# A gated mix of a spectral filter and a token MLP: mirrored filter rows read backwards by DMA, full-height matmuls, spectrum renumbered

## The chip, the cores and the metric

The kernel runs on one core of a Trainium2 chip. The metric is the device time of one execution in microseconds (us). The kernel before took 139.53 us, the median of three runs that lay between 139.4 and 141.93 us. The profile that is read below is of one execution of 138.61 us, of which 136.6 us are the span that the profile covers.

TensorE (PE) does the matmuls; "PEld" is its weight load, which runs beside the matmuls. VectorE (DVE) and ScalarE (ACT) do the element work. SyncE (SP) issues nearly all DMAs, and its queue of issues is called SPq. The DMAs run on 16 DMA engines.

## The reference: what is computed

The input x has 2048 tokens of 512 features. Three things are made of it and mixed:

```python
def _A_ref(x, w_r, w_i):                       # spectral filter
    X = rfft2(x)                               # 2048 x 257 complex
    X = X * (w_r + 1j * w_i)                   # w_r, w_i: 2048 x 257
    return irfft2(X, s=(2048, 512))

def _B_ref(x, w1, b1, w2, b2):                 # MLP over the tokens
    h = layernorm(x)                           # over the features
    u = gelu(einsum("bsd,sf->bdf", h, w1) + b1)     # 2048 -> 1792
    return (einsum("bdf,fs->bds", u, w2) + b2).transpose(0, 2, 1)

g = sigmoid((x * gate_w).sum(-1, keepdims=True))
out = g * _A_ref(x, A_w_r, A_w_i) + (1 - g) * _B_ref(x, ...)
```

## The kernel before

**A planner writes the order.** The kernel records tasks with `add(engine, duration, emit, reads, writes, prio, ...)`. Class `Plan` then simulates them with its own estimated durations and emits the instructions of every engine in the order that comes out. On the chip each engine works strictly through its own list, so the order is fixed, whatever the true times are. An instruction that waits holds up everything behind it in its engine's list.

**MLP.** The first matmul (`m1`, line 652) multiplies w1, which arrives in three parts: one of 6 column tiles (`wa`) and two of 4 column tiles (`wb`), each loaded by four DMAs. ACT applies gelu (line 666). The second matmul (`m2`, line 927) needs all 14 tiles of w2, which are loaded into the same buffers by seven DMAs of 1 MB. The m2 matmuls also fill PE's time around the spectral stages.

**Spectral filter.** The transform over the tokens is done by matmuls with cosine and sine tables (`fa`, lines 509 to 512) and radix-4 butterflies on DVE; the transform over the features by `fb` (lines 617 to 620), whose results ACT copies into `B` (line 624). Frequency k and its mirror 2048 - k are made from the same matmul results, so the filter is needed at both, side by side.

**The filter W.** `W` in SBUF holds 128 partitions x (real/imaginary, 2 kinds of rows `lt`, 4 blocks `e`, 2 places: computed and mirrored) x 257 values. `ld_W` loads the computed rows to their places. The mirrored rows run the other way, so they are loaded in forward order to a staging tile `wt`. PE then turns them with an anti-diagonal matrix (`wf`, line 702, 16 matmuls of 256 columns, and `wfn`, line 712, 4 small ones for the last column), and ACT copies them to `W` (lines 706 and 715). `wprep` on DVE (lines 722 to 726) waits for both components of W, and everything after it on DVE is in this order: small products (`c0b`), the butterfly `bfly` (765), a special line `nyq` (746 to 749), the multiplication by W (`mul`, 773), `comb`, `ob`, and the inverse radix-4 steps (548 to 564). Row 0 of the spectrum and the row at the Nyquist frequency are special and sit on partition 0; eight rows of them travel through a small matmul (`linem`, line 804).

**Inverse and output.** `i1` (lines 835 to 842) transforms back over the tokens, `i3` (lines 909 to 913) over the features. In both, one matmul of each group contracts a single row, from partition 0: line 841 (`d(1)[0:1]` against `ti[0:1]`, 4 times) and line 910 (`zv[0][0:1, 1]` against `g[0:1]`, 16 times). The bias matmuls (631, 633) contract 14 and 4 rows, and `linem` 9. ACT and DVE finish each group of 128 tokens, and SP stores it.

**Queues.** All loads of W, w1's second and third part and w2 stand in one queue, SP's, in this order: gate weights, W real (12 DMAs), the third part of w1 (4 DMAs of 512 KB), W imaginary (12 DMAs), the inverse table `ti`, the table `tg`, w2 (7 DMAs). SP uses eight DMA semaphores in turn: before it issues a DMA it waits until the one issued eight before has landed.

Of the kernel before, what the change touches and what calls it, by code (L numbers as in the profile page):

```python
# [16 lines left out]
P = 128  # L17
# [13 lines left out]

def ti_at(r):
    return (0, 1024, 512, 1920)[r], (512, 896)[r % 2]


def make_tables():
# [10 lines left out]
    for r in range(4):  # L47
        s = 4 * p + r
        for n, k0 in enumerate((0, 2)):
            th = ang(s, k0 + 4 * np.arange(64), S)  # L50
            ta[:, r, n * 128:n * 128 + 64] = np.cos(th)
            ta[:, r, n * 128 + 64:n * 128 + 128] = -np.sin(th)
        ta[:, r, 64] = alt
        th = ang(s, 1 + 4 * p, S)
        ta[:, r, 256:384] = np.cos(th)
        ta[:, r, 384:512] = -np.sin(th)
        ta[:, r, 512:640] = -np.cos(th)

        k = np.where(p < 64, 4 * p, 2 + 4 * (p - 64))
        o, w = ti_at(r)  # L60
        v = ti[:, o:o + w]
        if r % 2:
            sg = np.where(p < 64, 1.0, -1.0)[:, None]
# [6 lines left out]
            v[0, 2:4] = alt * (0.5 ** 0.5 if r == 1 else -(0.5 ** 0.5))  # L70
            th = ang(1 + 4 * p, s, S)
            v[:, 4] = -np.sin(th)
            v[:, 5] = np.cos(th)
            v[:, 6] = np.sin(th)
            ti[:, o:o + w] = v.reshape(P, w)
        else:
            s5 = np.append(s, 512)
            for lt, kk in enumerate((k, 1 + 4 * p)):
                th = ang(kk, s5, S)
                c, n = np.cos(th), -np.sin(th)  # L80
                if lt == 0:
                    n[0, 0:P] = 0.0 if r == 0 else -alt
# [4 lines left out]
    ti[0, 2816:2945] = np.append(alt, 1.0)  # L87
# [174 lines left out]
def kernel(  # L262
# [42 lines left out]
    def alloc_first():  # L305
# [8 lines left out]
        V.memset(t["warm"], 0.0)  # L314
        t["st"] = sb([P, 4096], BF16, "st")
        t["gl"] = sb([P, NFT, D], BF16, "gl")
        t["W"] = sb([P, 2, 2, 4, 2, WL], BF16, "W")
        t["wn"] = sb([1, 2, WL], BF16, "wn")
        t["ta"] = sb([P, 4, 640], BF16, "rot")
        t["wt"] = sb([P, 2, 2, 4, WL], BF16, "wt")  # L320
# [62 lines left out]
    def ld_bias():  # L383
        t["b1b"] = sb([NFT, P], BF16, "b1b")
        t["b2b"] = sb([4, D], BF16, "b2b")
        dma(t["b1b"][:], B_b1.rearrange("(t f) -> t f", f=P))
        dma(t["b2b"][:], B_b2.rearrange("(q n) -> q n", q=4))
    add("SP", 1.0, ld_bias, writes=["bias"], prio=7.1, nbytes=16384)
# [21 lines left out]
    def ld_W(comp):  # L410
        v = wsrc[comp].rearrange("(e c k) l -> c e k l", e=4, k=4)
        z = wsrc[comp].rearrange("(v u w) l -> w u v l", v=4, u=2)

        def emit():
            W, u = t["W"], t["wt"]
            dma(W[:, comp, 1, :, 0, 0:257], v[:, :, 1, :])
            dma(u[:, comp, 1, :, 0:257], v[:, :, 3, :])
            dma(W[1:64, comp, 0, :, 0, 0:257], v[1:64, :, 0, :])
            dma(W[64:128, comp, 0, :, 0, 0:257], v[0:64, :, 2, :])
            dma(u[64:127, comp, 0, :, 0:257], v[65:128, :, 0, :])  # L420
            dma(u[0:64, comp, 0, :, 0:257], v[64:128, :, 2, :])

            for i in range(2):
                dma(W[0:1, comp, 0, 2 * i:2 * i + 2, 0, 0:257], z[0:1, i, 0:2, :])
            dma(u[127:128, comp, 0, 0:2, 0:257], z[0:1, 1, 2:4, :])
            dma(u[127:128, comp, 0, 2, 0:257], wsrc[comp][1536:1537, :])
            dma(u[127:128, comp, 0, 3, 0:257], wsrc[comp][0:1, :])
            dma(t["wn"][:, comp, 0:257], wsrc[comp][1024:1025, :])
        return emit

    for comp in range(2):
        add("SP", 9.0 - 2 * comp, ld_W(comp), writes=[("W", comp), ("wt", comp)], prio=17 + 8 * comp, nbytes=300000, after=[a0])
        if comp == 0:
            load_wb(1)
# [8 lines left out]
    for r in range(4):  # L443
# [128 lines left out]
    def sp0():  # L572
        V.tensor_copy(t["sp"][:], t["X"][:, 0, :, :, :, 0])
# [25 lines left out]
    add("DVE", 0.15, lambda: V.tensor_copy(t["X"][:, 0, :, :, :, 0], t["fx"][:]), reads=["fx"],  # L599
# [94 lines left out]
    for comp in range(2):  # L694
        for lt in (1, 0):
            for a in range(2):
                tag = ("fa", "fb")[a]

                def wf(comp=comp, lt=lt, a=a, tag=tag):
                    pw = t["pw", comp, lt, a] = ps([P, 2, L], F32, tag, 2)  # L700
# [6 lines left out]
                add("ACT", act(512), wfe, reads=[("pw", comp, lt, a)], writes=[("W~", comp, lt)], prio=3, free=[tag])

    def wfn():
        pw = t["pwn"] = ps([P, 4, 4], F32, "fa", 2)  # L710
        for e in range(4):
            T.matmul(pw[:, e], lhsT=t["flip"][:], rhs=t["wt"][:, :, :, 3 - e, 256], start=True, stop=True)
    add("PE", mm(*[4] * 4), wfn, reads=[("wt", 0), ("wt", 1), "flip"], writes=["pwn"], prio=5, alloc=["fa"])
    wtk = [("W~", comp, lt) for comp in range(2) for lt in range(2)]
    add("ACT", 0.3, lambda: A.copy(t["W"][:, :, :, :, 1, 256].rearrange("p k a e -> p (k a) e"), t["pwn"][:].rearrange("p e k -> p k e")),
        reads=["pwn"], writes=wtk, prio=3, free=["fa"])

    pbk = [("pb", lt, e, c) for lt in range(2) for e in range(4) for c in range(2)]

    def wprep():  # L720
        W, pm = t["W"], t["wpm"]
        V.tensor_scalar_mul(W[0:1, :, 0, 0, :, 0:257], W[0:1, :, 0, 0, :, 0:257], 0.5)
# [4 lines left out]
    add("DVE", 0.8, wprep, reads=[], writes=[("W", 0), ("W", 1), "wpm"] + wtk, prio=1)  # L727


    for lt in range(2):  # L730
# [8 lines left out]
        if lt == 0:  # L739
            def nyq():  # L740
                pz = sb([1, 1280], F32, "X")
                na = pz[:, 0:1024].rearrange("p (i v l) -> p i v l", i=2, v=2)
                nn = t["nn"] = pz[:, 1024:1280].bitcast(BF16).rearrange("p (v l) -> p v l", v=2)
                wn, v = t["wn"], t["B"][0:1, 0, 0, 2:4, :]
# [4 lines left out]
                V.tensor_mul(nn[:, :, 0], t["c0"][0:1, 0, 0, 1, :], wn[:, 0, 0:257:256])  # L749
# [18 lines left out]
        for comp in range(2):  # L768
# [5 lines left out]
            add("DVE", tt(4096), mul, reads=["xs", ("W", comp), ("W~", comp, lt)], writes=[("pp", "st")[comp]], prio=pr)  # L774
# [19 lines left out]
        if lt == 0:  # L794
            def lines():
                t["s9"] = sb([9, D], BF16, "s9")
                t["s8"] = sb([8, D], BF16, "s8")
                dma(t["s9"][0:8], t["B"][0:1, 0].rearrange("p e (c v) l -> p (e c) (v l)", c=2))
# [9 lines left out]
    for lt in range(2):  # L808
# [5 lines left out]
        if lt == 0:  # L814
            add("SP", 0.5, lambda: dma(t["B"][0:1, 0].rearrange("p e (c v) l -> p (e c) (v l)", c=2), t["s8"][:]),
                reads=["s8"], writes=[("T", 0, 0), ("T", 0, 1)], prio=0, nbytes=8192)

    for h in range(2):
        for r in (0, 2, 1, 3):
            for lt in range(2):  # L820
                tag = ("fa", "fb")[lt]

                def i1(h=h, r=r, lt=lt, tag=tag):
                    if "zz" not in t:
                        t["zz"] = sb([P, 2, 2, 2, 2, 4, P], BF16, "X")
                        t["ze"] = sb([P, 2, 2, 2, 2, L], BF16, "wt")
# [3 lines left out]
                    for v in range(2):  # L830
# [5 lines left out]
                        else:  # L836
# [3 lines left out]
                            if n > P:  # L840
                                T.matmul(p1[:, v, 0:n], lhsT=d(1)[0:1], rhs=t["ti"][0:1, 2816:2945], start=False, stop=True)
# [58 lines left out]
    for grp in groups:  # L900
        for j in grp:
# [3 lines left out]
            def i3(j=j, q=q, r=r, tag=tag):  # L905
# [4 lines left out]
                T.matmul(p3[:, 0, 0:129], lhsT=zv[0][0:1, 1], rhs=g[0:1, 512:641], start=False, stop=True)  # L910
# [99 lines left out]
```

## Time and profile before

| what | value |
|---|---|
| median of three runs | 139.53 us |
| the profiled execution | 138.61 us |
| its span | 136.6 us |
| PE busy | 130.8 us (96%) |
| DVE busy | 114.6 us (84%) |
| ACT busy | 82.5 us (60%) |
| DMA | 23.18 MB, mean 170 GB/s |
| clock granted to PE | full in every stretch |

How to read the views that follow. The line with 40 digits gives the busy share of an engine in 40 equal slices of the span (3.4 us each), in tenths. The chain of work starts at the last instruction and goes back, at each step, to what released it; each piece has its start, its length and its line. A window row gives, for a stretch of the span, its length, the clock granted to PE (1.00 is full), the mean busy share of the 16 DMA engines, and GB/s. The share of the DMA engines can exceed 1 where packets of one engine overlap. In the list of groups, a matmul's "mean ns of one" is its latency; as matmuls are pipelined, the time that one costs PE is the distance from its start to the next start, which the chain shows.

### The profile page before, as it was taken

How to read it: one execution, taken by the hardware profiler on the slowest of the kernel's cores; microseconds unless marked ns; L12 is line 12 of the kernel's file. 1: busy time of each engine (PE TensorE's matmuls, PEld its weight loads, DVE VectorE, ACT ScalarE, POOL GpSimd, SP SyncE). 2: the span in 40 equal slices, each digit the busy share in tenths (PEclk: the TensorE clock that was granted, in tenths of full speed). 3: DMA queues.
4: the chain of work that ended last, by engine and by line, in shares of the span. 5: the costliest groups of instructions: out<-in, count | busy, mean ns of one | idle time of the engine just before them, and what ended most of it. 6: DMA issues, size and time to landing. Idle time of an engine off the chain costs nothing.

```text
span 136.6 us, 2166 instructions
## 1 busy us (share of the span) xinstructions
PE 130.8 (96%) x763; PEld 71.8 (53%) x777; DVE 114.6 (84%) x291; ACT 82.5 (60%) x159; POOL 0.2 (0%) x4
## 2 busy tenths in 40 slices
PE   6988999999999999999999999999999999999991
PEld 2353555445544857444445455557755545555590
DVE  0999999999999983699999999994885999949531
ACT  4066699999999999972220072259956457553200
POOL 0000000000000000000000000000000000000000
PEclk9999999999999999999999999999999999999999
DMA  4999999992899479999128600000000030303031
GB/s 124 318 376 362 361 364 349 332 166 42 243 348 258 81 255 281 413 409 404 47 19 350 247 0 5 2 2 0 0 0 5 0 154 14 139 5 154 6 112 38
DMA packets 17110, 23.18 MB, mean 170 GB/s; under 512 B 1078, under 2 KB 14540, under 8 KB 17100
## 3 DMA queue, kind: packets, MB, share of 16 engines
q1 hardware_dynamic: 16540, 22.39, 50.9%
q10 hardware_dynamic: 560, 0.66, 1.4%
q8 instruction: 6, 0.10, 0.3%
q14 instruction: 4, 0.03, 0.1%
HBM read 20.93 MB, written 2.10 MB: 169 GB/s over the span
## 4 chain that ended last, share of the span: by engine, by line
PE 62%; DMA 25%; SPq 9%; issue 1%; DVE 0%
PE acc L927 34%; PE acc L652 13%; DMA wa<-in_B_w_dram 11%; SPq L303 9%; DMA wt<-in_A_w_i_dram 8%; DMA wt<-in_A_w_r_dram 5%; PE fa L835 1%; PE fb L835 1%; PE fa L927 1%; PE fb L911 1%; PE fa L911 1%; PE fb L910 1%; PE fa L910 1%; PE fa L842 1%; PE fa L620 1%
## 5 line engine op out<-in xcount | busy, mean ns | idle before, releaser
L927 PE MATMUL acc<-gl,wb 128*128 128x512 bf16 (+1 forms) x123 | 30.9, 372 | 0.3
L652 PE MATMUL acc<-h,wb 128*128 128x512 bf16 x124 | 29.0, 379 | 0.1
L927 PE MATMUL acc<-gl,wa 128*128 128x512 bf16 (+1 forms) x94 | 23.4, 372 | 0.1
L947 ACT ACTIVATE x<-acc,ombb,omg 128x512 bf16<-128x512 f32 x14 | 10.7, 778 | 16.9 <-PE acc L927 16.9
L927 PEld LDWEIGHTS <-wb 128*128 128x128 bf16 x136 | 14.9, 114 | 9.9 <-issue 0.2
L652 PEld LDWEIGHTS <-wb 128*128 128x128 bf16 x128 | 12.4, 98 | 13.1
L652 PE MATMUL acc<-h,wa 128*128 128x512 bf16 x62 | 16.8, 379 | 1.0 <-DMA wa<-in_B_w_dram 0.5
L927 PEld LDWEIGHTS <-wa 128*128 128x128 bf16 x102 | 11.5, 114 | 8.8
L652 PEld LDWEIGHTS <-wa 128*128 128x128 bf16 x96 | 9.1, 98 | 10.1 <-DMA wa<-in_B_w_dram 0.6
L666 ACT ACTIVATE gl<-acc,b1f 128x512 bf16<-128x512 f32 x12 | 8.6, 715 | 8.4 <-PE acc L652 8.3
L458 DVE BATCH_NORM_STATS2 stats<-x 128x6 f32<-128x512 bf16 x16 | 10.7, 672 | 2.4 <-DMA x<-in_A_x_dram 2.4
L482 ACT ACTIVATE h<-x,nmr,rstd 128x512 bf16<-128x512 bf16 x13 | 9.8, 805 | 1.2 <-DVE nmr L473 1.2
L515 ACT CAST X<-fa 128x512 bf16<-128x512 f32 x16 | 8.8, 583 | 2.6 <-PE fa L512 2.5
L680 ACT ACTIVATE x<-x 128x512 bf16<-128x512 bf16 x16 | 10.2, 673 | 0.0
L652 PE MATMUL fb<-h,wa 128*128 128x512 bf16 x31 | 9.0, 379 | 0.0
L953 DVE TENSOR_TENSOR x<-x,eo 128x512 bf16<-128x512 bf16 x14 | 5.4, 418 | 2.7 <-ACT x L947 2.7
L348 PE MATMUL fa<-xp 128*128 128x512 bf16 x13 | 5.7, 632 | 1.2 <-DVE xp L314 1.2
L918 ACT ACTIVATE eo<-fa,g 128x512 bf16<-128x512 f32 x8 | 5.5, 686 | 2.1 <-PE fa L913 1.2
L918 ACT ACTIVATE eo<-fb,g 128x512 bf16<-128x512 f32 x8 | 5.5, 688 | 0.0
L806 ACT CAST s<-fa 8x512 bf16<-8x512 f32 x1 | 0.6, 575 | 7.8 <-PE fa L804 7.8
L624 ACT CAST B<-fb 128x512 bf16<-128x512 f32 x8 | 5.3, 661 | 0.0
L624 ACT CAST B<-fa 128x512 bf16<-128x512 f32 x8 | 5.2, 650 | 0.0
(164 smaller groups left out, 235.5 us busy)
## 6 DMA issues: line engine op xcount, KB each, us to landing
wb<-in_B_w_dram SPq DMA_DIRECT2D x8, 512.0 KB
wb<-in_B_w_dram SPq DMA_DIRECT2D x4, 1024.0 KB
wa<-in_B_w_dram SPq DMA_DIRECT2D x3, 1024.0 KB
wa<-in_B_w_dram SPq DMA_DIRECT2D x3, 768.0 KB
x<-in_A_x_dram SPq DMA_DIRECT2D x3, 512.0 KB
out_dram<-x SPq DMA_DIRECT2D x3, 512.0 KB
rot<-dft_ti SPq DMA_DIRECT2D x1, 736.5 KB
rot<-dft_ta SPq DMA_DIRECT2D x4, 160.0 KB
```

The lines of the kernel that those rows point to most:

```text
L303: (eng or nc.sync).dma_start(out=out_ap, in_=in_ap)
L348: T.matmul(pw[:], lhsT=t["warm"][:, 0:P], rhs=t["warm"], start=True, stop=True)
L458: V.bn_stats(out=t["stats"][:, j, :], in_=t["x"][:, j // 4, j % 4, :])
L482: add("ACT", act(512, 2), lambda j=j: A.activation(t["h"][:, j // 4, j % 4, :], t["x"][:, j // 4, j % 4, :], ActF.Identity, bias=t["nmr"][ ...
L515: add("ACT", act(512), lambda r=r, dq=dq: A.copy(t["X"][:, :, r, :, dq, :], t["pa", r, dq][:]), reads=[("pa", r, dq)], writes=[("X", r, dq ...
L624: A.copy(t["B"][:, lt, e, 2 * c:2 * c + 2, :].rearrange("p s (i b) -> p s i b", b=4), t["pb", lt, e, c][:].rearrange("p s b i -> p s i b"))
L652: T.matmul(t["u", ft][:], lhsT=w[:, j // 4, j % 4, c * P:(c + 1) * P], rhs=t["h"][:, j // 4, j % 4, :], start=(j == jorder[0]), stop=(j == ...
L666: gelus.append(add("ACT", act(512, 1), lambda ft=ft: A.activation(t["gl"][:, ft, :], t["u", ft][:], ActF.Gelu_apprx_tanh, bias=t["b1f"][:, ...
L680: A.activation(t["x"][:, q, r, :], t["x"][:, q, r, :], ActF.Copy, accum_out=t["glog"][:, 4 * q + r:4 * q + r + 1])
L918: A.activation(t["eo", j][:], t["i3", j][:], ActF.Copy, scale=t["g"][:, j:j + 1])
L927: T.matmul(t["y", j, n][:, cs], lhsT=w[:, o, 512 * q + r:512 * q + 512:4], rhs=t["gl"][:, ft, cs], start=(ft == 0), stop=(ft == NFT - 1))
L947: A.activation(tbuf(j).rearrange("p h d -> p (h d)"), t["y", j, 0][:], ActF.Identity, bias=t["ombb2"][:, j:j + 1], scale=t["omg"][:, j:j + 1])
```

## The change

Four edits go together.

1. **The mirrored rows are read backwards by DMA into their place.** `wt`, the 20 turning matmuls and the 9 ACT copies are gone. `ld_W` now issues four loads of 63 or 64 rows by 4 blocks, and eight loads of 128 rows whose source is written as 2 groups of 64 rows with a negative step (`"(o i) l -> o i l", o=2` and `[:, ::-1]`; `"(i q) l -> q i l", q=4` and `[0:4:2, ::-1]`). In the built program the source of such a load is [2 entries][64 rows, step -4 rows][257 values] and its destination [128 partitions][257 values]. There are 16 DMAs for each component in `ld_W` where there were 12, and two more for each component (`special`), which write two rows at partition 64 over what the backward loads put there. In SP's list these stand behind `ti` and `tg`, and the last two behind the first 1 MB of w2.
2. **The spectrum is renumbered**, so that a backward run of rows starts on partition 0 or 64: the tables are made for the new numbering (`KA`, `KB`, `p ^ 64`), and the special row moves from partition 0 to 64.
3. **Full-height matmuls.** The matmuls that contracted 1, 4, 9 or 14 rows contract all 128; the other rows of the operands are zero, for which three tiles are cleared at the start (`s9`, `b1b`, `b2b`, three DVE memsets).
4. `ze`, which lived in the staging tile's memory, has memory of its own.

```diff
+        t["s9"] = sb([P, D], BF16, "s9")
+        t["b1b"] = sb([P, P], BF16, "b1b")
+        t["b2b"] = sb([P, D], BF16, "b2b")
+        for k in ("s9", "b1b", "b2b"):
+            V.memset(t[k][:], 0.0)
...
         def emit():
-            W, u = t["W"], t["wt"]
-            dma(W[:, comp, 1, :, 0, 0:257], v[:, :, 1, :])
-            dma(u[:, comp, 1, :, 0:257], v[:, :, 3, :])
-            dma(W[1:64, comp, 0, :, 0, 0:257], v[1:64, :, 0, :])
-            dma(W[64:128, comp, 0, :, 0, 0:257], v[0:64, :, 2, :])
-            dma(u[64:127, comp, 0, :, 0:257], v[65:128, :, 0, :])
-            dma(u[0:64, comp, 0, :, 0:257], v[64:128, :, 2, :])
...
+            W, src = t["W"][:, comp], wsrc[comp]
+            dma(W[0:64, 1, :, 0, 0:257], v[64:128, :, 1, :])
+            dma(W[64:128, 1, :, 0, 0:257], v[0:64, :, 1, :])
+            dma(W[0:64, 0, :, 1, 0:257], v[64:128, ::-1, 2, :])
+            dma(W[65:128, 0, :, 1, 0:257], v[65:128, ::-1, 0, :])
+            for e in range(4):
+                dma(W[:, 1, e, 1, 0:257], v[:, 3 - e, 3, :].rearrange("(o i) l -> o i l", o=2)[:, ::-1])
+                dma(W[:, 0, e, 0, 0:257], src[512 * e + 2:512 * e + 258, :].rearrange("(i q) l -> q i l", q=4)[0:4:2, ::-1])
+            dma(W[64:65, 0, 1:3, 1, 0:257], z[0:1, 0:2, 3, :])
...
+        def special():
             for i in range(2):
-                dma(W[0:1, comp, 0, 2 * i:2 * i + 2, 0, 0:257], z[0:1, i, 0:2, :])
...
+                dma(t["W"][64:65, comp, 0, 2 * i:2 * i + 2, 0, 0:257], z[0:1, i, 0:2, :])
+        return emit, special
...
+        add("SP", 9.0 - 2 * comp, emit, writes=[("W", comp)], prio=17 + 8 * comp, nbytes=300000, after=[a0])
+        add("SP", 1.0, special, writes=[("W", comp)], prio=29.5, nbytes=4112)
...
-                    for i in range(2):
-                        T.matmul(pw[:, i], lhsT=t["flip"][:], rhs=t["wt"][:, comp, lt, 3 - 2 * a - i, 0:L], start=True, stop=True)
...
-                    A.copy(t["W"][:, comp, lt, 2 * a:2 * a + 2, 1, 0:L], t["pw", comp, lt, a][:])
...
-                T.matmul(pl8[:], lhsT=t["tb"][0:9, 1152:1160], rhs=t["s9"][:], start=True, stop=True)
+                T.matmul(pl8[:], lhsT=t["tb"][:, 1152:1160], rhs=t["s9"][:], start=True, stop=True)
...
-                                T.matmul(p1[:, v, 0:n], lhsT=d(1)[0:1], rhs=t["ti"][0:1, 2816:2945], start=False, stop=True)
+                                T.matmul(p1[:, v, 0:n], lhsT=d(1), rhs=t["ti"][:, 2816:2945], start=False, stop=True)
...
-                T.matmul(p3[:, 0, 0:129], lhsT=zv[0][0:1, 1], rhs=g[0:1, 512:641], start=False, stop=True)
+                T.matmul(p3[:, 0, 0:129], lhsT=zv[0][:, 1], rhs=g[:, 512:641], start=False, stop=True)
```

More of the change, by code (lines that the diff above doesn't have):

```diff
@@ L29, in bf @@
     return np.ascontiguousarray(a.astype(ml_dtypes.bfloat16))
+KA = np.append(0, 256 - 4 * np.arange(1, 64))
+KB = 254 - 4 * np.arange(64)
 def ti_at(r):
@@ L48, in make_tables @@
         s = 4 * p + r
-        for n, k0 in enumerate((0, 2)):
-            th = ang(s, k0 + 4 * np.arange(64), S)
+        for n, kk in enumerate((KA, KB)):
+            th = ang(s, kk, S)
             ta[:, r, n * 128:n * 128 + 64] = np.cos(th)
@@ L53, in make_tables @@
         ta[:, r, 64] = alt
-        th = ang(s, 1 + 4 * p, S)
+        th = ang(s, 1 + 4 * (p ^ 64), S)
         ta[:, r, 256:384] = np.cos(th)
@@ L57, in make_tables @@
         ta[:, r, 512:640] = -np.cos(th)
-        k = np.where(p < 64, 4 * p, 2 + 4 * (p - 64))
+        k = np.append(KB, KA)
         o, w = ti_at(r)
@@ L62, in make_tables @@
         if r % 2:
-            sg = np.where(p < 64, 1.0, -1.0)[:, None]
+            sg = np.where(p < 64, -1.0, 1.0)[:, None]
             th = ang(k, s, S)
@@ L69, in make_tables @@
             v[:, 3] = -sg * np.sin(th)
-            v[0, 2:4] = alt * (0.5 ** 0.5 if r == 1 else -(0.5 ** 0.5))
-            th = ang(1 + 4 * p, s, S)
+            v[64, 2:4] = alt * (0.5 ** 0.5 if r == 1 else -(0.5 ** 0.5))
+            th = ang(1 + 4 * (p ^ 64), s, S)
             v[:, 4] = -np.sin(th)
@@ L77, in make_tables @@
             s5 = np.append(s, 512)
-            for lt, kk in enumerate((k, 1 + 4 * p)):
+            for lt, kk in enumerate((k, 1 + 4 * (p ^ 64))):
                 th = ang(kk, s5, S)
@@ L81, in make_tables @@
                 if lt == 0:
-                    n[0, 0:P] = 0.0 if r == 0 else -alt
+                    n[64, 0:P] = 0.0 if r == 0 else -alt
                 u = v[:, 256 * lt:256 * lt + 256]
@@ L86, in make_tables @@
                     u[:, P] = c[:, P] if lt == 0 else -n[:, P]
-    ti[0, 2816:2945] = np.append(alt, 1.0)
+    ti[64, 2816:2945] = np.append(alt, 1.0)
     tb = np.zeros((P, 3, 4, 64))
@@ L317, in alloc_first @@
         t["W"] = sb([P, 2, 2, 4, 2, WL], BF16, "W")
-        t["wn"] = sb([1, 2, WL], BF16, "wn")
+        t["wn"] = sb([P, 2, WL], BF16, "wn")
         t["ta"] = sb([P, 4, 640], BF16, "rot")
-        t["wt"] = sb([P, 2, 2, 4, WL], BF16, "wt")
         t["wpm"] = sb([P, 2, 2, 4, 2], F32, "wpm")
@@ L383, in ld_bias @@
     def ld_bias():
[L384 to L388, printed above, removed]
+        dma(t["b1b"][0:NFT], B_b1.rearrange("(t f) -> t f", f=P))
+        dma(t["b2b"][0:4], B_b2.rearrange("(q n) -> q n", q=4))
+    add("SP", 1.0, ld_bias, writes=["bias"], prio=7.1, nbytes=16384, after=[a0])
     load("tb", [P, 1160], BF16, tabs["tb"], 296960, prio=9)
@@ L414, in emit @@
         def emit():
-            W, u = t["W"], t["wt"]
-            dma(W[:, comp, 1, :, 0, 0:257], v[:, :, 1, :])
-            dma(u[:, comp, 1, :, 0:257], v[:, :, 3, :])
-            dma(W[1:64, comp, 0, :, 0, 0:257], v[1:64, :, 0, :])
-            dma(W[64:128, comp, 0, :, 0, 0:257], v[0:64, :, 2, :])
-            dma(u[64:127, comp, 0, :, 0:257], v[65:128, :, 0, :])
-            dma(u[0:64, comp, 0, :, 0:257], v[64:128, :, 2, :])
-            for i in range(2):
-                dma(W[0:1, comp, 0, 2 * i:2 * i + 2, 0, 0:257], z[0:1, i, 0:2, :])
[L425 to L429, printed above, removed]
+            W, src = t["W"][:, comp], wsrc[comp]
[7 more added lines that the diff above has]
+            dma(W[64:65, 0, 1:3, 1, 0:257], z[0:1, 0:2, 3, :])
+            dma(W[64:65, 0, 0, 1, 0:257], src[0:1, :])
+            dma(W[64:65, 0, 3, 1, 0:257], src[1280:1281, :])
+            dma(t["wn"][64:65, comp, 0:257], src[1024:1025, :])
+        def special():
+            for i in range(2):
+                dma(t["W"][64:65, comp, 0, 2 * i:2 * i + 2, 0, 0:257], z[0:1, i, 0:2, :])
+        return emit, special
     for comp in range(2):
-        add("SP", 9.0 - 2 * comp, ld_W(comp), writes=[("W", comp), ("wt", comp)], prio=17 + 8 * comp, nbytes=300000, after=[a0])
+        emit, special = ld_W(comp)
+        add("SP", 9.0 - 2 * comp, emit, writes=[("W", comp)], prio=17 + 8 * comp, nbytes=300000, after=[a0])
+        add("SP", 1.0, special, writes=[("W", comp)], prio=29.5, nbytes=4112)
         if comp == 0:
@@ L510, in fa @@
                 T.matmul(pa[:, 1], lhsT=w(3), rhs=ta[:, 384:640], start=False, stop=True)
-                T.matmul(pa[:, 0, :, 0:64], lhsT=w(0), rhs=ta[:, 0:128], start=True, stop=True)
-                T.matmul(pa[:, 0, :, 64:128], lhsT=w(1), rhs=ta[:, 128:256], start=True, stop=True)
+                T.matmul(pa[:, 0, :, 64:128], lhsT=w(0), rhs=ta[:, 0:128], start=True, stop=True)
+                T.matmul(pa[:, 0, :, 0:64], lhsT=w(1), rhs=ta[:, 128:256], start=True, stop=True)
             add("PE", mm(128, 128, 256, 256), fa, reads=[("xf", r % 2), ("ta", r)], writes=[("pa", r, dq)], prio=0, alloc=["fa"],
@@ L572, in sp0 @@
     def sp0():
-        V.tensor_copy(t["sp"][:], t["X"][:, 0, :, :, :, 0])
+        V.tensor_copy(t["sp"][:], t["X"][:, 0, :, :, :, 64])
     dk = [("D", r) for r in range(4)]
@@ L598 @@
                dk + ([] if lt else ["sp"]), [("Z", lt, 0), ("Z", lt, 1)], pr, False)
-    add("DVE", 0.15, lambda: V.tensor_copy(t["X"][:, 0, :, :, :, 0], t["fx"][:]), reads=["fx"],
+    add("DVE", 0.15, lambda: V.tensor_copy(t["X"][:, 0, :, :, :, 64], t["fx"][:]), reads=["fx"],
         writes=[("Z", 0, 0), ("Z", 0, 1)], prio=3.1)
@@ L630, in biasT @@
         pb = t["pbias"] = ps([P, 32], F32, "fa", 2)
-        T.matmul(pb[:, 0:NFT], lhsT=t["b1b"][:], rhs=t["flip"][0:NFT, P - NFT:P], start=True, stop=True)
+        T.matmul(pb[:, 0:NFT], lhsT=t["b1b"][:], rhs=t["flip"][:, P - NFT:P], start=True, stop=True)
         for r in range(4):
-            T.matmul(pb[:, 16 + 4 * r:20 + 4 * r], lhsT=t["b2b"][:, r::4], rhs=t["flip"][0:4, P - 4:P], start=True, stop=True)
+            T.matmul(pb[:, 16 + 4 * r:20 + 4 * r], lhsT=t["b2b"][:, r::4], rhs=t["flip"][:, P - 4:P], start=True, stop=True)
     add("PE", 0.3, biasT, reads=["bias", "flip"], writes=["pbias"], prio=9, alloc=["fa"])
@@ L692 @@
     add("SP", 0.2, ld_ti, writes=["ti"], prio=28, nbytes=754176, after=[pl.last_w["pa", r, dq] for r in range(4) for dq in range(4)])
[L694 to L700, printed above, removed]
-                    for i in range(2):
-                        T.matmul(pw[:, i], lhsT=t["flip"][:], rhs=t["wt"][:, comp, lt, 3 - 2 * a - i, 0:L], start=True, stop=True)
-                add("PE", mm(256, 256), wf, reads=[("wt", comp), "flip"], writes=[("pw", comp, lt, a)], prio=5, alloc=[tag])
-                def wfe(comp=comp, lt=lt, a=a):
-                    A.copy(t["W"][:, comp, lt, 2 * a:2 * a + 2, 1, 0:L], t["pw", comp, lt, a][:])
[L707 to L716, printed above, removed]
     pbk = [("pb", lt, e, c) for lt in range(2) for e in range(4) for c in range(2)]
@@ L721, in wprep @@
         W, pm = t["W"], t["wpm"]
-        V.tensor_scalar_mul(W[0:1, :, 0, 0, :, 0:257], W[0:1, :, 0, 0, :, 0:257], 0.5)
+        V.tensor_scalar_mul(W[64:65, :, 0, 0, :, 0:257], W[64:65, :, 0, 0, :, 0:257], 0.5)
         ends = [W[:, comp].rearrange("p a e s l -> p (a e) s l")[:, :, :, 0:257:256] for comp in range(2)]
@@ L726, in wprep @@
         V.tensor_sub(pv[1], ends[1][:, :, 0], ends[1][:, :, 1])
-    add("DVE", 0.8, wprep, reads=[], writes=[("W", 0), ("W", 1), "wpm"] + wtk, prio=1)
+    add("DVE", 0.8, wprep, reads=[], writes=[("W", 0), ("W", 1), "wpm"], prio=1)
     for lt in range(2):
@@ L740, in nyq @@
             def nyq():
-                pz = sb([1, 1280], F32, "X")
+                pz = sb([P, 1280], F32, "X")[64:65]
                 na = pz[:, 0:1024].rearrange("p (i v l) -> p i v l", i=2, v=2)
                 nn = t["nn"] = pz[:, 1024:1280].bitcast(BF16).rearrange("p (v l) -> p v l", v=2)
-                wn, v = t["wn"], t["B"][0:1, 0, 0, 2:4, :]
+                wn, v = t["wn"][64:65], t["B"][64:65, 0, 0, 2:4, :]
                 for i in range(2):
@@ L748, in nyq @@
                 V.tensor_add(nn[:, 1], na[:, 1, 1], na[:, 0, 0])
-                V.tensor_mul(nn[:, :, 0], t["c0"][0:1, 0, 0, 1, :], wn[:, 0, 0:257:256])
+                V.tensor_mul(nn[:, :, 0], t["c0"][64:65, 0, 0, 1, :], wn[:, 0, 0:257:256])
             add("DVE", 3 * d1(512) + 0.1, nyq, reads=bk + [("W", 0), ("W", 1), ("c0", 0)] + pbk, writes=["nn"], prio=0.5)
@@ L773, in mul @@
                 V.tensor_mul(o, xs, w)
-            add("DVE", tt(4096), mul, reads=["xs", ("W", comp), ("W~", comp, lt)], writes=[("pp", "st")[comp]], prio=pr)
+            add("DVE", tt(4096), mul, reads=["xs", ("W", comp)], writes=[("pp", "st")[comp]], prio=pr)
         def comb(lt=lt):
@@ L795, in lines @@
             def lines():
[L796 removed]
                 t["s8"] = sb([8, D], BF16, "s8")
[L798 removed]
+                dma(t["s9"][0:8], t["B"][64:65, 0].rearrange("p e (c v) l -> p (e c) (v l)", c=2))
                 dma(t["s9"][8:9], t["nn"].rearrange("p v l -> p (v l)"))
@@ L814 @@
         if lt == 0:
-            add("SP", 0.5, lambda: dma(t["B"][0:1, 0].rearrange("p e (c v) l -> p (e c) (v l)", c=2), t["s8"][:]),
+            add("SP", 0.5, lambda: dma(t["B"][64:65, 0].rearrange("p e (c v) l -> p (e c) (v l)", c=2), t["s8"][:]),
                 reads=["s8"], writes=[("T", 0, 0), ("T", 0, 1)], prio=0, nbytes=8192)
@@ L825, in i1 @@
                         t["zz"] = sb([P, 2, 2, 2, 2, 4, P], BF16, "X")
-                        t["ze"] = sb([P, 2, 2, 2, 2, L], BF16, "wt")
+                        t["ze"] = sb([P, 2, 2, 2, 2, L], BF16, "ze")
                     p1 = t["i1", h, r, lt] = ps([P, 2, L], F32, tag, 2)
```

## The prediction

> **What bounds the kernel now.** I read the slices first, then the chain, then the loads of W in windows, then DVE after them.
>
> ```profile
> PE   6988999999999999999999999999999999999991
> DVE  0999999999999983699999999994885999949531
> DMA  4999999992899479999128600000000030303031
> ```
>
> PE is full from 10 us to the end, at full clock: the end is set by the sum of what PE does, so long as its fixed list never waits. DVE has one hole, in the two slices from 51 us: before it can start on the filter it waits for W.
>
> ```profile
> 103.03 0.06 PE fa L909
> 103.08 0.16 PE fa L910
> 103.24 0.16 PE fa L911
> ...
> 103.52 0.06 PE fb L909
> ```
>
> In the chain (start, length, line) a 129-column matmul costs 0.06 us; the one-row matmul of line 910 costs 0.16, and so does its full-height successor in line 911.
>
> ```profile
> 27.00:28.00 1.00, 1.00 1.22 276
> 28.00:29.00 1.00, 1.00 1.16 141
> 29.00:30.00 1.00, 1.00 1.12 171
> 30.00:31.00 1.00, 1.00 0.94 110
> 31.00:32.00 1.00, 1.00 0.38 69
> 32.00:33.00 1.00, 1.00 0.15 37
> ...
> 37.00:38.00 1.00, 1.00 1.09 379
> ```
>
> These windows (length, PE clock, DMA share, GB/s) show W's real part arriving. From 28 to 33 us, 528 KB move, which is the 1016 rows of 514 bytes of the two 63-row and two 64-row loads. The rows do not spread evenly: from 31 us on 0.38 and then 0.15 of 16 engines, 6.1 and 2.4 engines, still work while the others are empty. The shape of a load decides on how many engines it runs: 63 rows cannot be dealt out in 16 equal parts.
>
> ```profile
> 47.98 0.43 SPq L303 DMA_DIRECT2D tg<-dft_tg  x1
> 48.51 1.67 SPq L303 DMA_DIRECT2D wa<-in_B_w_dram  x3
> ```
>
> ```profile
> 52.87 0.42 DVE L722 TENSOR_SCALAR W<-W 1x1028 bf16<-1x1028 bf16 x1 [2.04 <-ACT W L715]
> ```
>
> ```profile
> 89.96 0.06 PE fa L839
> ```
>
> From the timelines of SP and DVE and from the chain: SP has issued the last of W when `tg` goes out at 47.98; `wprep` starts at 52.87; 37.1 us later, at 89.96, the inverse `i1` starts on PE. Between them DVE stands idle for 1.5 us only (two waits for `B`, 1.2 and 0.3 us).
>
> **The change, part by part.**
>
> *One-row matmuls.* At full height lines 910 and 911 should cost 0.06 each, 0.20 us less for a pair: 16 pairs give 3.2 us, the four of lines 841 and 842 0.8 us. Together 4.0 us, all behind 89.96. The bias and `linem` matmuls are six; at most 0.1 us.
>
> *Turning on PE and ACT.* The chain has a pair of L702 at 0.22 us: 8 pairs 1.8 us, and 0.09 for L712. The nine ACT copies (about 0.7 us each) go too. All this lies before 52 us.
>
> *DVE memsets.* Three at the start; the one of 256 words takes 0.27 us, so under 1 us, hidden in DVE's first wait of 2.4 us for x.
>
> *The loads of W.* This decides. As many rows as before come in, but per component 1020 of them by four loads that deal out like the old ones (64 and 63 rows), and 1024 by eight loads whose source has an outer count of 2. No such load of 128 rows is in the trace. From one side it runs on 16 engines like the old 128-row loads, from the other on 2, half of the rows on each. I take two: a count of 63 visibly kept loads from 16 engines, and 2 is the outermost count here.
>
> The Trainium skill bears on this, against the change: "DMA: Bandwidth & Descriptors", section "Why a DMA increments its semaphore by 16 and not by 1", says that a load runs on the largest number of engines up to 16 that divides the slowest dimension of both patterns. That would be 9 for 63 rows, as the tail of the windows suggests, and 2 here, always the same lowest two; by 16 engines the sum would be the second rival's.
>
> What does a row cost one engine? Where 2.4 engines were busy (32 to 33 us), each moved 37 / 2.4 = 15.4 GB/s, 33 ns a row; at 31 us 69 / 6.1 = 11.3 GB/s, 45 ns. Slowest reading: nine engines carried 56 rows of the 63-row loads and 32 of the others from 28.0 to 33.2 us, 59 ns. Fastest: the best slice of the page, 413 GB/s over 16 engines, 20 ns. I take 33 ns, from the window nearest to two engines.
>
> The two engines then work in order, as all these loads stand in one queue:
> - Start: the old 128-row loads of real W (1024 rows, 64 per engine, 2.1 us) were through by 28.0, so W begins at 25.9.
> - Four plain loads: up to 48 + 28 = 76 rows, 2.5 us: 28.4.
> - Eight backward loads: 512 rows each, 16.9 us: 45.3.
> - Third part of w1: 4 x 32 KB per engine at 379 / 16 = 23.7 GB/s, 5.5 us: 50.8. PE needs it at about 52: a wait of 1 to 3 us.
> - Imaginary W: 2.5 + 16.9 us: 70.2.
> - `ti`, `tg` and the first 1 MB of w2 (120 KB per engine, 5.1 us: 75.3), because the last `special` rows stand behind them in SP's list; about 2 us to land (`B<-s`, issued by 87.91, freed line 839 at 89.96): 77.3.
>
> So `wprep` starts at 77.3, not 52.87. SP's twelve extra issues (about 0.65 us each) vanish in its waits on the semaphore of eight before. Queued behind are w2 (7 MB, 18 us at 400 GB/s, complete by 93) and all of DVE's list.
>
> *What is late next.* DVE's stretch from `wprep` to `i1` is 37.1 - 1.5 = 35.6 us, as `B` is long ready: `i1` at 112.9. PE runs out of work at about 73 us (the first w2 matmul was at 70.2), gets w2 piecemeal, and stands until 112.9; its gain before that is lost. From `i1` to the end of the span: 136.6 - 89.96 - 4.0 = 42.6 us, since the matmuls behind `i1` stay behind it in PE's list. Span 155.5; with the 2.0 us around the span 157.5, against the profiled 138.61. The runs' median is 0.9 above that execution: 158.4, and I forecast 159, the rest for a gap or two between loads.
>
> The skill's "TensorE: Matmul & The Clock Gate", Part 1, adds that an idle PE falls to half clock until some 3.4 us of work have passed; the trace, with PE never idle, cannot show it. By it the start of `i1` would cost an estimated 1.7 us more.
>
> **Rivals.**
>
> *Same mechanism, slower rows (45 to 59 ns).* Each engine has 2 x (512 + 76) = 1176 rows, so 1 ns a row moves the end by 1.2 us: 12 ns more give 173, 26 ns more 190. For it: the 31 us window and the landing at 33.2. Against: there up to nine engines wrote into few partitions at once. *Faster rows (20 to 30 ns)* give 144 to 155; only loads with longer rows moved at that rate.
>
> *The backward loads spread over 16 engines: faster.* Place: the eight loads per component. Price: then W is through by about 48 as now, the last `special` lands behind 1 MB of w2 (4 us) at about 53, and `i1` starts at 90 again. PE saves 4.0 us behind it: 132.6 + 2.0 = 134.6, and 1.8 us from the turning become idle time. If DVE (15.15 us busy of 17 from 103 to 120) cannot follow, 137 to 139. It decides as soon as the engines per load are more than two by enough that W is in by 53; at two engines even 20 ns a row leaves `wprep` at 62, nine us late. For it: 128 rows stand on the destination's side.
>
> *Full height does not remove the 0.16 us:* 4 us on top of any case.
>
> **How the numbers follow.** Two engines at 30 to 45 ns a row, 155 to 173: 0.62. Slower rows, 173 to 190: 0.15. Faster rows, 144 to 155: 0.10. Spread loads: 0.13, of which 0.08 faster and 0.05 within 2%. A difference of 2% is about what runs of this kernel can tell from none (they spread from 139.4 to 141.93). The range 146 to 183 leaves out the spread loads and the ends of the other two.
>
> **What would show it.** Right: DMA digits of 1 or 2 at 30 to 60 GB/s in two stretches of some 17 us (about 28 to 45 and 53 to 70); `wprep` waiting for a DMA until about 77; PE empty in places from 73 to 113; lines 910 and 911 at 0.06 in the chain; full DVE for 36 us from `wprep`. Wrong: W complete by 50 with DMA digits of 9, or a backward load that takes much less than 64 x 33 ns = 2.1 us; then the answer is the spread case.

## The result and the profile after

The changed kernel took 159.45 us, the median of four runs (157.18 to 159.83), beside 140.11 us for the kernel before in four runs. The ratio is 1.131, with a 95% interval of 1.109 to 1.154: slower. Ratios here are taken over the runs that lie near the fastest of each kernel, so they can differ from the ratio of the medians beside them. The profiled execution took 159.64 us, with a span of 157.8 us.

The slices of the changed kernel's page, each 3.9 us long:

```profile
PE   6889999999999500000599999999999999999991
DVE  3989999999999000000319999999994968999981
PEclk9999999999999975555579999999999999999999
DMA  5999999611179711179994007600000000303321
```

PE was full to the end before. Now it has one hole, from 53 to 77 us, and is full again behind it; DVE's hole lies in the same place. DMA has two stretches of the digit 1, one per component of W. PE's clock falls to half in the hole.

The windows of the changed kernel (length, PE clock, DMA share, GB/s):

```profile
31.00:42.00 11.00, 1.00 0.15 38
46.00:48.00 2.00, 1.00 1.08 360
55.00:67.00 12.00, 0.60 0.15 37
56.00:57.00 1.00, 1.00 0.16 36
57.00:58.00 1.00, 0.67 0.15 37
58.00:59.00 1.00, 0.50 0.15 36
...
81.00:82.00 1.00, 0.88 1.03 422
```

A share of 0.15 is 2.4 of 16 engines, as in the one window of the kernel before where the other engines were empty. The share counts packets that overlap, so it is no count of engines. The trace also keeps the semaphore updates that DMAs make as they land: in this kernel a two-group load has two, a 63-row load nine, and in the kernel with one run of 128 rows (below) each such load has sixteen. That fits two engines per two-group load. Between the two stretches the third part of w1 passes at 360 GB/s.

SyncE's timeline of the changed kernel (start, length, what is issued):

```profile
22.00 20.61 SPq L307 DMA_DIRECT2D W<-in_A_w_r_dram  x15
...
42.95 3.16 SPq L307 DMA_DIRECT2D wb<-in_B_w_dram  x4
46.15 19.80 SPq L307 DMA_DIRECT2D W<-in_A_w_i_dram  x15
...
66.74 0.43 SPq L307 DMA_DIRECT2D tg<-dft_tg  x1
67.21 2.42 SPq L307 DMA_DIRECT2D W<-in_A_w_r_dram  x2
69.73 0.39 SPq L307 DMA_DIRECT2D wa<-in_B_w_dram  x1
70.17 1.17 SPq L307 DMA_DIRECT2D W<-in_A_w_i_dram  x2
```

`tg` goes out at 66.74, where it went out at 47.98 before, and the `special` rows (the `x2` lines) stand behind it, the last two also behind 1 MB of w2. DVE's timeline shows when they have landed, and what else stood in DVE's list:

```profile
74.64 0.42 DVE L708 TENSOR_SCALAR W<-W 1x1028 bf16<-1x1028 bf16 x1 [23.64 <-DMA W<-in_A_w_i_dram]
...
76.29 0.24 DVE L609 CAST X<-fx 128x32 bf16<-128x32 f32 x1
81.91 0.17 DVE L722 CAST c<-B 128x8 f32<-128x8 bf16 x1 [5.38 <-ACT B L634]
```

`wprep` (line 708 now) waited 23.64 us for W. The copy in line 609, which has nothing to do with W, ran only after it. It writes part of `X`, which `fb` needs. PE's timeline:

```profile
47.88 5.56 PE L662 MATMUL acc<-h,wb 128*128 128x512 bf16 x24
76.59 0.29 PE L627 MATMUL fa<-tb,X 128*128 128x128 bf16 x1 [23.15 <-DVE X L609]
```

So what stopped PE is not W but this copy, queued behind the instruction that waits for W. Behind PE's wait stood the rest of the first MLP matmul, which needs neither.

The chain, past the hole:

```profile
117.19 0.06 PE fa L824
117.25 0.06 PE fa L826
117.30 0.06 PE fa L827
...
129.47 0.06 PE fa L894
129.52 0.06 PE fa L895
```

Line 826 is the former one-row matmul of `i1` (line 841 before), line 895 that of `i3` (line 910 before): 0.06 each now, and no 0.16 for it or its successor.

**The account of the 21.2 us.** PE's busy time went from 130.8 to 127.4 us (-3.4), its idle time from 5.8 to 30.4 us (+24.6). Together +21.2, the difference of the spans (157.8 - 136.6). The hole at line 627 is 23.2 of the idle time. The busy time fell by 4.0 for the one-row matmuls and by some 1.9 for the turning, and rose by about 2.2 because seven groups of `fb` ran at half clock, 0.64 us each instead of 0.33; that is -3.7, and the other 0.3 us stays open.

### The profile page after: what moved, and what is told of

It reads as the page before. It is cut to its first block, busy times and chain, and to the rows that moved or that the text cites. A ratio compares the mean times of both kernels' runs of the same rounds, so it can differ in the third digit from the quotient of the medians.

```text
span 157.8 us, 2131 instructions
## 1 busy us (share of the span) xinstructions
PE 127.4 (81%) x743; PEld 71.2 (45%) x757; DVE 115.1 (73%) x294; ACT 79.4 (50%) x150; POOL 0.2 (0%) x4
## 4 chain that ended last, share of the span: by engine, by line
DMA 30%; PE 29%; SPq 20%; DVE 16%; ACT 2%; issue 2%; DVEq 0%; ACTq 0%
PE acc L912 20%; SPq L307 20%; DMA W<-in_A_w_i_dram 7%; DMA x<-in_A_x_dram 6%; DMA wb<-in_B_w_dram 5%; DMA W<-in_A_w_r_dram 4%; DMA wa<-in_B_w_dram 4%; DMA s<-X 3%; DVE xp L759 1%; DVE st L759 1%; DVE x L938 1%; ACT eo L903 1%; PE fa L820 1%; PE fb L820 1%; DVE eo L920 1%
## 5 line engine op out<-in xcount | busy, mean ns | idle before, releaser
L662 PE MATMUL acc<-h,wb 128*128 128x512 bf16 x124 | 27.9, 379 | 0.2
L627 PE MATMUL fa<-tb,X 128*128 128x128 bf16 x8 | 2.1, 263 | 23.2 <-DVE X L609 23.2
L634 ACT CAST B<-fa 128x512 bf16<-128x512 f32 x8 | 4.9, 608 | 24.5 <-PE fa L630 24.4
L627 PEld LDWEIGHTS <-X 128*128 128x128 bf16 x16 | 2.0, 122 | 24.3 <-DVE X L609 23.6
```

The costliest lines, as they stand in the source:

```text
L634: A.copy(t["B"][:, lt, e, 2 * c:2 * c + 2, :].rearrange("p s (i b) -> p s i b", b=4), t["pb", lt, e, c][:].rearrange("p s b i -> p s i b"))
L662: T.matmul(t["u", ft][:], lhsT=w[:, j // 4, j % 4, c * P:(c + 1) * P], rhs=t["h"][:, j // 4, j % 4, :], start=(j == jorder[0]), stop=(j == ...
```

## The experiments

Each kernel is compared with runs of the kernel before that were made beside it; the medians of these were 139.74, 140.01 and 139.65 us. In all kernels with forward loads the mirrored part of the filter stands in the wrong order; they serve for their times alone. The theory to be tested: the backward loads run on two engines because their source has an outermost count of 2; W is late by that; and two things set what the delay costs, DVE's stretch behind `wprep` and the copy queued behind it.

### Is it the count or the backward step?

First two groups read forward:

```diff
-  dma(W[:, 1, e, 1, 0:257], v[:, 3 - e, 3, :].rearrange("(o i) l -> o i l", o=2)[:, ::-1])
-  dma(W[:, 0, e, 0, 0:257], src[512*e+2:512*e+258, :].rearrange("(i q) l -> q i l", q=4)[0:4:2, ::-1])
+  dma(W[:, 1, e, 1, 0:257], v[:, 3 - e, 3, :].rearrange("(o i) l -> o i l", o=2))
+  dma(W[:, 0, e, 0, 0:257], src[512*e+2:512*e+258, :].rearrange("(i q) l -> q i l", q=4)[0:4:2])
```

> The eight mirrored loads per component keep their source of 2 groups of 64 rows, but the rows go forward; the mirrored part of the filter is then in the wrong order, and all else is as in the changed kernel. Theory (the outer count of 2 confines a load to two engines): the same as the changed kernel, two stretches at 36 to 40 GB/s, line 708 at 73 to 77 us, time 156 to 161. Rival (the negative step makes the loads slow): loads at over 250 GB/s, line 708 at 53 to 56, time 133 to 138.

It took 146.9 us. The edit did not do what was meant: without the negative step the two groups of the first line lie one behind the other, and in the built program they had become one run of 128 rows. Only four loads per component kept two groups. Theory and rival both failed: `wprep` waited 11.3 us, between the two cases, so this run decides nothing by itself. It was repeated with groups that can't be joined (every second row):

```diff
+  dma(W[:, 1, e, 1, 0:257], v[:, 3 - e, 3, :].rearrange("(i o) l -> o i l", o=2))
```

> All eight mirrored loads per component with a source of 2 groups of 64 forward rows that cannot be joined to one run (the groups interleave); the mirrored part of the filter is in the wrong order, all else as in the changed kernel. Theory (two engines for an outer count of 2, whatever the direction): two stretches at 36 to 40 GB/s, line 708 at 73 to 77 us, time 156 to 161. Rival (the negative step): as the run with one run of 128 rows, line 708 at 58 to 62, time 142 to 145.

160.02 us in one run. The windows and DVE's timeline of this kernel, whose loads have two groups and no backward step:

```profile
32.00:43.00 11.00, 1.00 0.16 40
55.00:67.00 12.00, 0.63 0.15 36
```

```profile
74.44 0.42 DVE L708 TENSOR_SCALAR W<-W 1x1028 bf16<-1x1028 bf16 x1 [23.50 <-DMA W<-in_A_w_i_dram]
```

The same stretches at the same rate, and `wprep` within 0.2 us of the changed kernel's. The backward step costs nothing that shows here; the two groups alone, read forward, give the whole delay.

### What would loads on all engines give?

The same eight loads as one run of 128 rows each:

```diff
+  dma(W[:, 1, e, 1, 0:257], v[:, 3 - e, 3, :])
+  dma(W[:, 0, e, 0, 0:257], src[512*e+2:512*e+258, :].rearrange("(n t) l -> n t l", t=2)[:, 0])
```

> The same eight loads of the same 128 rows each, but with a source of one run of 128 forward rows; the mirrored part of the filter is then in the wrong order, and all else is as in the changed kernel. Theory (engines follow the outer count): W moves at over 250 GB/s, line 708 starts at 53 to 56 us where it was 74.6, the inverse 38 us after it, time 134 to 137, faster than the kernel before by 2 to 4%. Rival (the loads or the special rows behind the inverse table are late for another reason): over 145.

143.46 us in four runs, ratio 1.024 (1.019 to 1.030). That is 16.0 us less than the changed kernel, but the prediction's price for this case, 134.6, was 9 us too low, and the expectation above, 134 to 137, missed as well. From SyncE's timeline and DVE's:

```profile
22.50 13.51 SPq L307 DMA_DIRECT2D W<-in_A_w_r_dram  x15
...
39.02 13.95 SPq L307 DMA_DIRECT2D W<-in_A_w_i_dram  x15
```

```profile
60.64 0.42 DVE L708 TENSOR_SCALAR W<-W 1x1028 bf16<-1x1028 bf16 x1 [8.90 <-DMA W<-in_A_w_i_dram]
```

Fifteen issues take 13.5 us, 0.9 us each with the waits between them, while the DMA engines are half empty (from 31 to 36 us: share 0.47, 99 GB/s). Either the issuing itself holds W up, 0.43 us for a load of 128 rows in the chain, or SyncE's wait until the DMA eight before has landed. Both depend on the number of loads, and so the four blocks were put into one load, ten loads per component instead of sixteen:

```diff
+  y = src.rearrange("(e n) l -> n e l", e=4)
+  dma(W[:, 1, :, 1, 0:257], v[:, ::-1, 3, :])
+  dma(W[:, 0, :, 0, 0:257], y[2:257:2])
```

> As the run with one run of 128 forward rows, but the four blocks of a kind come in one load, so that a component has 10 loads in place of 16 (mirrored rows again in the wrong order). Theory (with the engines free, SP's issues of some 0.65 to 0.85 us each are what W waits for): 6 issues less per component, W some 4 us earlier per component, line 708 at 52 to 55 us where it was 59.8, time 135 to 138. Rival (the rows themselves take that long, or the special rows behind w2 do): line 708 at 57 or later, 141 to 144.

139.52 us in ten runs that spread from 135.94 to 140.27, ratio 0.980 (0.975 to 0.986); the medians alone would give 0.997. Six of the ten lie above the expected range, at 139.4 or more, so the gain in time is left open, and the reading rests on the timelines. (In the kept trace of the run before, line 708 stands at 60.64, not at the expectation's 59.8.) SyncE's and DVE's timelines:

```profile
22.71 8.62 SPq L307 DMA_DIRECT2D W<-in_A_w_r_dram  x9
...
36.16 8.28 SPq L307 DMA_DIRECT2D W<-in_A_w_i_dram  x9
```

```profile
54.51 0.42 DVE L708 TENSOR_SCALAR W<-W 1x1028 bf16<-1x1028 bf16 x1 [2.71 <-DMA W<-in_A_w_i_dram]
```

The same rows and bytes in nine issues take 8.6 and 8.3 us, and `wprep` starts 6.1 us earlier. So the number of loads was what held W up. Its two effects can be told apart by SyncE's waits. With sixteen loads it waits for parts of w1 that were issued earlier (total, times, longest):

```profile
SPq L307 <- DMA wb<-in_B_w_dram: 10.5, 4, 3.0
```

With ten loads these waits are 1.5 us in all. Of the 27.5 us of the first kernel's two stretches, 15.5 are issuing; of the 16.9 us of the second's, 14.4 are. So the issuing fell by 1.1 us only, and most of the 10.6 us saved is SyncE's wait for an earlier DMA to land.

### What does the copy behind `wprep` cost?

The changed kernel, with one priority changed, so that the planner puts the copy ahead of `wprep`:

```diff
     add("DVE", 0.15, lambda: V.tensor_copy(t["X"][:, 0, :, :, :, 64], t["fx"][:]), reads=["fx"],
-        writes=[("Z", 0, 0), ("Z", 0, 1)], prio=3.1)
+        writes=[("Z", 0, 0), ("Z", 0, 1)], prio=0.5)
```

> The changed kernel with the small copy of line 609 given a planner priority ahead of wprep, so that the forward feature matmuls of the first kind of rows need not wait for W. Loads of W as in the change. Theory (the copy behind wprep in DVE's list held PE for 23 us and then B late): line 708 still at 74 to 77 us, no wait of PE on line 609, the inverse starts 35.6 to 37 us after line 708, time 151 to 155. Rival (the late W alone sets the end, B would have been late anyway): 157 to 160.

153.82 us in four runs, ratio 1.097 (1.091 to 1.103): 5.6 us less than the changed kernel, with W no earlier. DVE's and PE's timelines of this kernel:

```profile
51.88 0.24 DVE L609 CAST X<-fx 128x32 bf16<-128x32 f32 x1
...
75.99 0.42 DVE L708 TENSOR_SCALAR W<-W 1x1028 bf16<-1x1028 bf16 x1 [23.88 <-DMA W<-in_A_w_i_dram]
```

```profile
75.98 1.04 PE L912 MATMUL acc<-gl,wa 128*128 128x512 bf16 x2 [5.69 <-DMA wa<-in_B_w_dram]
...
111.03 0.22 PE L824 MATMUL fa<-rot,B 128*128 128x129 bf16 x1 [2.23 <-DMA B<-s]
```

PE no longer waits for the copy. It works through the first MLP matmul until 70.3 us, then gets w2 piecemeal (12.4 us of waits in all), and `i1` starts 35.0 us after `wprep`, held by DVE's chain. PE's clock is at half here too, from 74 to 91 us, so the 5.6 us are what is left when two such losses are set against each other. This is close to the picture that the prediction drew: it had 73 us, w2 piecemeal and 35.6 us.

### What is each part worth alone?

The kernel before with nothing but the two one-row matmuls at full height:

```diff
- T.matmul(p1[:, v, 0:n], lhsT=d(1)[0:1], rhs=t["ti"][0:1, 2816:2945], start=False, stop=True)
+ T.matmul(p1[:, v, 0:n], lhsT=d(1), rhs=t["ti"][:, 2816:2945], start=False, stop=True)
- T.matmul(p3[:, 0, 0:129], lhsT=zv[0][0:1, 1], rhs=g[0:1, 512:641], start=False, stop=True)
+ T.matmul(p3[:, 0, 0:129], lhsT=zv[0][:, 1], rhs=g[:, 512:641], start=False, stop=True)
```

> The kernel before with nothing changed but lines 841 and 910, which contract all 128 rows (zeros in the table's other rows). Theory: 20 pairs at 0.20 us less, 4.0 us: ratio 0.970 to 0.975, lines 910 and 911 at 0.06 us in the chain. Rival (VectorE, 15.15 us busy of 17 there, takes over): the matmuls do get shorter, but the time falls by only 1 to 2.5 us, ratio 0.982 to 0.993.

136.82 us in six runs, ratio 0.975 (0.970 to 0.980). By the medians that is 2.9 us, by the ratio 3.6 us, of the 4.0 us that 20 pairs at 0.20 us give. The chain of this kernel has all three matmuls at 0.06:

```profile
104.86 0.06 PE fa L909
104.92 0.06 PE fa L910
104.97 0.06 PE fa L911
```

Then the merged forward loads again, with the `special` rows issued ahead of w2 and the copy's priority raised. If removing the turning has a worth of its own, this kernel must lie below the one just shown:

```diff
...
-        add("SP", 1.0, special, writes=[("W", comp)], prio=29.5, nbytes=4112)
+        specials.append(add("SP", 1.0, special, writes=[("W", comp)], prio=29.5, nbytes=4112))
-        add("SP", 0.5, ldw2, reads=[("w2a", k)], writes=[("w2", i)], prio=31 + i, nbytes=1048576)
+        add("SP", 0.5, ldw2, reads=[("w2a", k)], writes=[("w2", i)], prio=31 + i, nbytes=1048576, after=specials)
...
-        writes=[("Z", 0, 0), ("Z", 0, 1)], prio=3.1)
+        writes=[("Z", 0, 0), ("Z", 0, 1)], prio=0.5)
```

> The merged loads, and in addition the special rows ahead of the first load of w2 in SP's list and the small copy of line 609 ahead of wprep (mirrored rows in the wrong order). Theory (these two orders and the loads are all that stands against the gain of the change): line 708 at 50 to 53 us, no wait of PE over 1 us after 10 us, time 133 to 135.5, below height_only's 136.8. Rival (the turning was free, and VectorE sets the end): 136 to 138.

136.63 us in four runs, ratio 0.976 (0.969 to 0.982): a miss, above the expected range by 1.1 us, inside its rival's, and level with the full-height kernel (136.82). `wprep` started at 52.75, as early as before, but here the planner put the copy behind it all the same, and PE waited 2.5 us for it, so this run does not show that the turning was free.

### Can the backward loads be kept?

The eight loads per component issued by GpSimd instead of SyncE:

```diff
-  dma(W[:, 1, e, 1, 0:257], v[:, 3 - e, 3, :].rearrange("(o i) l -> o i l", o=2)[:, ::-1])
+  dma(W[:, 1, e, 1, 0:257], v[:, 3 - e, 3, :].rearrange("(o i) l -> o i l", o=2)[:, ::-1], nc.gpsimd)
...
```

> The changed kernel with its eight backward loads per component issued by GpSimd in place of SP; they have nothing ahead of them there and start at once. All is computed as in the reference. Theory: if that queue gives each load two other engines, W's mirrored rows come in during the first 30 us beside the other loads, line 708 at 50 to 57 us, time 137 to 143. Rival: it uses the same two engines each time; then these two hold up x and w1 as well, PE waits in the first 40 us, time 155 to 175.

148.84 us in four runs, ratio 1.065 (1.058 to 1.072), outside both expected ranges. W was no longer late, `wprep` did not wait for a DMA. But GpSimd had nothing ahead of it and issued from 1.3 us on; x came late, and DVE's statistics waited 11.7 us for it (2.1 us in the changed kernel):

```profile
15.68 0.69 DVE L468 BATCH_NORM_STATS2 stats<-x 128x6 f32<-128x512 bf16 x1 [5.91 <-DMA x<-in_A_x_dram]
26.20 0.69 DVE L468 BATCH_NORM_STATS2 stats<-x 128x6 f32<-128x512 bf16 x1 [4.24 <-DMA x<-in_A_x_dram]
```

The last kernel starts them later: `back` issues the eight loads on GpSimd, and they write over two small clears that DVE makes after a statistic of the last group of x (`mv` 11). It also has the `special` rows ahead of w2 and the copy ahead of `wprep`. Beside it ran the full-height kernel again, on the same chip:

```diff
...
+    def touch():
+        V.memset(t["W"][:, :, 1, :, 1, 256], 0.0)
+        V.memset(t["W"][:, :, 0, :, 0, 256], 0.0)
+    touched = add("DVE", 0.15, touch, writes=["touch"], prio=-2, after=[pl.last_w["mv", 11]])
+    for comp in range(2):
+        back, special = backs[comp]
+        backt = add("POOL", 8.0, back, writes=[("W", comp)], prio=0, after=[touched])
...
```

> The changed kernel with three edits: the eight backward loads of each component are issued by GpSimd, and only from the middle of the x statistics' last group on (about 24.4 us, after two small DVE clears that the loads write over); the special rows are issued ahead of w2; the copy of line 609 has priority ahead of wprep. Nothing is left out. If an early start was all that was wrong with GpSimd's queue (x and w1 held up), the 16 issues last about 16 x 1.0 us, W is in by about 45, wprep starts by 51 as in the kernel before, and the time is that of the kernel with full-height matmuls alone, 135 to 138. If the two-group loads run on the same two engines on this queue too, they move 38 GB/s, 28 us for both components, W is in at about 54 or later, and the time is 140 to 146. If removing the turning on TensorE is worth its 1.8 us, the time lies below 135.5.

> The kernel before with lines 841 and 910 at full height, beside the delayed GpSimd loads on the same chip: 0.970 to 0.979 of the kernel before, about 136.5 us. If it is the faster of the two by over 1 us, the backward loads cost something even off the path; if the other one is, the turning on TensorE was worth removing.

136.45 us, ratio 0.980 (0.973 to 0.988), against 136.92 us, ratio 0.975 (0.963 to 0.988), four runs each. GpSimd's and DVE's timelines and two windows of the kernel with the delayed loads:

```profile
26.29 6.43 POOL L307 DMA_DIRECT2D W<-in_A_w_r_dram  x8 [25.84 <-DVE nmr L487]
35.05 4.86 POOL L307 DMA_DIRECT2D W<-in_A_w_i_dram  x6 [2.33 <-DMA W<-in_A_w_r_dram]
```

```profile
57.38 0.42 DVE L721 TENSOR_SCALAR W<-W 1x1028 bf16<-1x1028 bf16 x1 [4.38 <-DMA W<-in_A_w_i_dram]
```

```profile
36.00:40.00 4.00, 1.00 1.17 213
44.00:48.00 4.00, 1.00 1.19 152
```

So the whole change can be had without its loss, 23 us faster than as it was made, and the DMA engines are full while the two-group loads run. W came later than expected (`wprep` at 57.4, not 51), but the copy now stands ahead of it, and PE never waits long. Yet it does not beat the kernel before with two lines changed: the medians differ by 0.5 us, well inside both intervals. The work that the turning took from PE is gone here (PE busy 126.6 us, against 128.2 in the full-height kernel beside it), and nothing measurable came of it. Part of it may have gone into two waits of 0.6 and 0.5 us that PE has at `i1`, for `B`; whether an earlier W would bring it out was not tried.

## Why the prediction was right

The forecast of 159 against 159.45 us is right in its direction and in the part of its mechanism that decides: two engines per backward load, and so a W that is late by 21.8 us (forecast 24.4). The way from W to the end ran otherwise. The forecast had PE empty in places from 73 to 113 us, waiting for w2 and for `i1`; in the run PE stands still from 53 to 77 us, for the copy, and is full after that. That the sum is right to half a microsecond is in part luck: errors of opposite sign cancelled. Step by step:

- **Two engines per backward load: right.** The two stretches at a share of 0.15 and the two updates per load show it, and the two-group forward loads show that the count is the cause. The rule of the Trainium skill ("DMA: Bandwidth & Descriptors", "Why a DMA increments its semaphore by 16 and not by 1") that was weighed against the change holds in these runs: 36 to 40 GB/s for two groups on SyncE's queue.
- **33 ns per row: too much.** It came from dividing 37 GB/s by 2.4 engines. The share overstates the engines: with two, 38 GB/s is 19 GB/s each, 27 ns for 514 bytes. SyncE's steps agree, about 1.7 us from one backward load's issue to the next in the chain, 64 rows at 27 ns. The stretches lasted some 13 us each where 16.9 were forecast. As the first one also began later, W's imaginary part was in at 69.1 us against 70.2.
- **The last `special` rows behind `ti`, `tg` and 1 MB of w2: right.** They landed at 74.6, forecast 77.3.
- **Third part of w1 late by 1 to 3 us: not seen.** PE stood at line 627 before it could meet that wait, and in the kernel with the copy first it did not wait for w1 either.
- **35.6 us from `wprep` to `i1`, "as `B` is long ready": this step failed.** The forecast looked at what W's products wait for, and not at what else stands behind `wprep` in DVE's list. The copy of line 609 did, `fb` waited for it, and `B`, made from `fb`, was not there: 5.4 and 0.4 us of waiting on DVE that the forecast had put at nothing, and 42.6 us from `wprep` to `i1`. The end is now set by PE's own work after its hole, since from 103.3 us until `i1` PE runs without a wait. With the copy moved, the step comes out: 35.0 us.
- **From `i1` to the end 42.6 us:** 40.6 in the run. Together: 155.5 - 2.7 (W) + 7.0 (copy) - 2.0 = 157.8, the measured span.
- **One-row matmuls, 0.20 us a pair: right** in the chain. Alone they give 2.9 to 3.6 of the forecast's 4.0 us; the intervals reach 4.0.
- **1.8 us of turning that go:** the forecast counted them as idle time in the case of spread loads, and the delayed loads agree as far as they go.
- **Half clock in the hole: right.** The clock fell at 57.3 us, 3.9 us after PE stopped at 53.4, and was back at 81.2, 4.7 us after PE went on at 76.6. The skill's figure ("TensorE: Matmul & The Clock Gate", Part 1) is a window of about 3.4 us for both; both took longer here. It was to cost an estimated 1.7 us and cost about 2.2, at another place than forecast.
- **The rival "spread over 16 engines", 134.6 us: a wrong price.** It took the loads' time for the transfer's alone and let SyncE's twelve extra issues "vanish in its waits". With sixteen loads per component SyncE was at W for 13.5 us, 7.0 of issuing and 5.8 of waiting one after the other, and the run took 143.5. Only with fewer loads, or with half of them on another queue, did the time come down to between 136 and 140.

## What to carry to other kernels

Look at the outermost count of a load's source and destination before its bytes: eight loads of 64 KB with a count of 2 took 13 us, in which the 360 GB/s beside them moves 4.7 MB. When an instruction will wait longer than before, list what stands behind it on its engine and who waits for each entry, however small it is: one 0.24 us copy cost 5.6 us. And weigh each part of a combined change alone: two lines of this one held all of its measurable gain.

## What was not expected of the hardware

- Two-group loads issued by GpSimd are not confined as those issued by SyncE are: 152 to 213 GB/s at a share of 1.2 while they run beside other loads, against 38 GB/s at 0.15. The skill's page on DMA, in the section named above, says that on that queue each load takes its engines from a cursor that moves round, and not always the lowest; the windows agree, but they do not show the engines one by one, so that each load ran on more than two engines is not excluded. Each such issue took GpSimd about 0.8 us.
- Backward rows of 514 bytes move no slower than forward ones in the same two groups (38 and 40 GB/s).
- Loads that differ from each other by a negative step alone can differ in shape: without it two neighbouring groups were joined to one, and the load has sixteen updates in its trace, where a two-group load has two.
